# Attention run ahead of the weights, chunk six spread behind the last weights, and the products of chunks four and five gathered by batch

## The chip, the cores and the metric

One Trainium2 chip, of which the kernel uses one core. A core has a matrix engine (TensorE; PE in the profile, PEld for its weight loads), VectorE (DVE), ScalarE (ACT), GpSimd (POOL), and SyncE (SP), which here only issues transfers. They run side by side and wait for each other through semaphores; 16 DMA engines move data between main memory and the on-chip memory. POOL issues all loads here, since they convert float32 to 16 bits on the way; SP issues the rest. The metric is device time in microseconds (us) for one execution.

## The reference

A causal attention with a cumulative bias, and on its result a spectral mixing layer with 64 complex weight matrices. B = 8 batches, H = 8 heads, S = 576 tokens, head width 64, model width 512:

```python
scores = scale * np.matmul(q, k.transpose(0, 1, 3, 2))
cum = np.cumsum(np.maximum(s, 0.0), axis=-1)
bias = -(cum[:, :, :, None] - cum[:, :, None, :])
scores = np.where(causal, -1e9, scores + np.minimum(bias, 0.0))
attn = softmax(scores)
x = heads_side_by_side(np.matmul(attn, v))        # [8, 576, 512]

X = np.fft.rfft(x, axis=1)                        # 64 modes are kept
Yr = einsum('bmd,mde->bme', Xr, w_r) - einsum('bmd,mde->bme', Xi, w_i)
Yi = einsum('bmd,mde->bme', Xr, w_i) + einsum('bmd,mde->bme', Xi, w_r)
y = np.fft.irfft(Y, n=S, axis=1)
u = x + y
return u + np.maximum(u @ w_ch, 0.0)
```

The two weight tensors w_r and w_i are 64 x 512 x 512 each, 134 MB together in float32; q, k and v are 9.4 MB each. The output is 9.4 MB.

## The kernel before, in words

**Steps and groups.** Attention runs in 32 steps (line 591). Step n takes two heads (group n // 8, 128 of the 512 columns) of batch n % 8: `scores` (lines 391 and 397 on TensorE, the exponentials of line 405 and, for the last 64 tokens, 376 on ScalarE), `av` (line 433, normalised into x_all in line 443), and `fft`, the forward transform of the step's columns into 64 modes (line 458), copied to `xs` (line 468). The next step's q and k are transposed on the way (line 355, copies of line 359).

**Units and chunks.** The weights come in 64 units: a group's 128 rows of eight modes of w_r or of w_i, 1.05 MB on chip, two loads of 512 KB (the very last unit four of 256 KB). A chunk is the two units of eight modes: 32 chunks, eight for each of the four groups. `modes` multiplies a chunk (line 478): 16 products, four at a time side by side in the array; the sums over the groups gather in y_acc. The last group's eight chunks are called chunk zero to chunk seven below (24 to 31 of 32 in all); their sum is y for eight modes, 16 rows (real and imaginary) of each batch. A chunk needs attention to have finished its group for all eight batches.

**Where the weights wait.** The first four units lie in space that is used later for other things. From then on two rings hold them: five buffers (WA) and three (WB), the ring of three only up to unit 37 (LW2). A unit's load waits until the chunk that last used its buffer is multiplied. `on_chip` says how many half units are asked for by step n, and `mode_steps` in which step which chunk is multiplied. POOL issues the loads strictly in the order of the program: step n asks for v of step n + 3, for q and k of steps n + 3 and n + 4 in odd steps, and for weights, evenly mixed (`load`, line 244). In `before` 51 units are asked for by step 31, and 24 chunks are multiplied during attention. Counted off from the program:

| by step | 8 | 16 | 24 | 31 |
|---|---|---|---|---|
| units asked for, before | 12 | 24 | 40 | 51 |
| chunks multiplied before that step, before | 0 | 8 | 16 | 23 |

**Behind attention.** The remaining chunks are multiplied as their units land. Beside them the kernel works ahead on the product x @ w_ch. The output is made in 18 pairs of 128-token tiles. For 16 of them (`kept`) x @ w_ch is stored: the tile is transposed (line 669, copied by DVE in line 673), multiplied with w_ch (line 682) and stored by ScalarE (line 539). `work` does one transposition of a pair and the product and storing of the pair before; `TAKE` says how many turns of it come after which chunk. In `before`, six of these pairs (`first_pairs`) are done earlier, in attention's steps 26 to 31 (lines 548, 553, 571), and ten behind it: three, two and three turns after chunks zero, one and two, and two inside the first gather; the last pair is kept in the middle of chunk six.

**From y to the inverse transform.** The inverse transform needs, for each batch, the 128 mode rows of y and of v = y @ w_ch below each other, in `yv`; y itself leaves `modes` with eight batches mixed in its rows. Two ways lead there. `gather` does it with TensorE: the transposed y (line 702) times an identity (for y) or times w_ch (for v), separately for each batch, and copies from the accumulators by ScalarE and VectorE (lines 739 and 741). The other way is `spread` (line 513), a transfer of SP, 128 KB. In `before` chunks zero to three are gathered after chunk three, both y and v, in four rounds of two batches; y of chunks four and five is gathered after chunk five, in two rounds of four batches; v of four and five (multiplied for all batches at once in line 710) and y and v of six and seven are spread.

**The end.** While chunk seven's last unit arrives, `first_z` and `first_u` begin the first two pairs; chunks six and seven enter these pairs directly (line 785), for all others they come from yv. Then the list of steps at the end of the function finishes the 18 pairs in an order written out by hand: products of line 774 and 804, a ReLU or copy on ScalarE (825, 827), sums on DVE and POOL, outputs by SP.

SP's queue holds in order: small loads of bias rows in attention, constants, the spreads, the outputs.

Of the kernel before, what the change touches and what calls it, by code (L numbers as in the profile page):

```python
# [10 lines left out]
FP32 = mybir.dt.float32  # L11
# [8 lines left out]
def kernel(  # L20
# [83 lines left out]

    xs = [gp.tile([P, 2, 2, 2, 2, B, HM], BF16, name=f"xs{i}") for i in range(2)]
    xs_flat = [t.rearrange("p q k h r b m -> p (q k h r b m)") for t in xs]
# [9 lines left out]

    dpool = ctx.enter_context(tc.tile_pool(name="dram", bufs=1, space=bass.MemoryType.DRAM))
    ncum_dram = dpool.tile([NPAIR, S + HP], BF16, name="ncum_dram")
    at = ExitStack()
# [128 lines left out]
    NW = 2  # L248
    mode_steps = {B: [0, 1, 2, 3], B + 1: [4], B + 2: [5], B + 4: [6], B + 6: [7]}
    for c in range(NCK, (NG - 1) * NCK):  # L250
        mode_steps.setdefault(B + c - (0 < c % NCK < 4), []).append(c)
    used = [NW * sum(len(cs) for t, cs in mode_steps.items() if t < n) for n in range(N + 1)]
    W0 = 2
    on_chip = []
    for n in range(N):
        w = 4 + 2 * (WA + WB + NE - 2) * (n + 1) // (B + 1) if n < B else plan + (3 if n <= 2 * B else 4)
        plan = w

        nt, ring = 0, ([], [])
        while nt < min(w // 2, len(wq)):  # L260
            i = ring_of(nt)
            if i is not None:
                depth = (WA, WB)[i]
                if len(ring[i]) >= depth and ring[i][-depth] >= used[n]:
                    break
                ring[i].append(nt)
            nt += 1
        if nt < w // 2:
            plan = 2 * nt + 1
        on_chip.append(2 * nt)  # L270

# [178 lines left out]
    def fft(n):  # L450
# [13 lines left out]
        for h in range(2):  # L464
            for q_ in range(2):
                a = ps[HP * q_ : HP * q_ + HP, h, : 2 * HM].rearrange("p (r m) -> p r m", r=2)
                a = bass.AP(tensor=a.tensor, offset=a.offset, ap=[a.ap[0], [HM, 2]] + list(a.ap[1:]))
                nc.vector.tensor_copy(out=xs[g % 2][HP * h : HP * h + HP, q_, :, h, :, b, :], in_=a)  # L468

    def modes(g, c, meanwhile=None):  # L470


        ps = auxpool.tile([P, DM], FP32, name="yp", tag="aux")
        cols = xs[g % 2].rearrange("p q k h r b m -> p q k (h r b) m")

# [21 lines left out]
        elif g < NG - 1:  # L497
            nc.vector.tensor_tensor(out=y_acc[:, c, :], in0=ps, in1=y_acc[:, c, :], op=ALU.add)  # L498
        else:
            yb = spool.tile([P, DM], FP16, name="y_sb", tag="y")  # L500
            for cols in halves if c == NCK - 1 else [slice(0, DM)]:
                nc.vector.tensor_tensor(
                    out=yb[:, cols], in0=ps[:, cols], in1=y_acc[:, c, cols], op=ALU.add
                )
            if c >= NCK - 2:
                spread(c, 0, yb)
            return yb
# [18 lines left out]

    first_pairs = [i for i in kept[1:] if pairs[i][0][1] < NF and pairs[i][0][0] <= 4][:6]
    z1s, xts1 = {}, {}

# [13 lines left out]

    def first_transposed(i, x):
        b, T = pairs[i][x]
        ps = auxpool.tile([P, DT, P], FP32, name="xt_ps", tag="aux")
        for dt in range(DT):
            nc.tensor.matmul(
                ps[:, dt, :], x_all[:, dt, b, T, :], ident16h, start=True, stop=True,
                skip_group_check=True,  # L550
            )
        xts1[i, x] = spool.tile([P, DT, P], FP16, name="xt1", tag="yt")
        nc.vector.tensor_copy(out=xts1[i, x], in_=ps)

    open_unit = {}

    def half_of(pool, name):
# [6 lines left out]
        return t[:, :HU]  # L564

    def first_product(i, x):
        if x == 0:
            kept_place(i, half_of(wpool2, "z1"))
        ps = auxpool.tile([P, DM], FP32, name="z1_ps", tag="aux")
        for dt in range(DT):  # L570
            nc.tensor.matmul(
                ps, xts1[i, x][:, dt, :], wch_sb[:, dt, :], start=(dt == 0), stop=(dt == DT - 1)
            )
        keep_product(i, x, ps)


# [5 lines left out]
    with tc.tile_pool(name="sc_psum", bufs=2, space=PSUM) as scpool, \  # L582
# [8 lines left out]
        for n in range(N):  # L591
            if n in (0, 2):
                nc.vector.memset(xs_flat[n // 2].bitcast(FP32), 0.0)
# [18 lines left out]
            scores(n, 1)  # L612
            i = first_pairs[n - N + len(first_pairs)] if n >= N - len(first_pairs) else None
            if i is not None:
                first_transposed(i, 0)
            transposes(n + 1, 1)
            fft(n - 1)
            av(n, 0)
            if i is not None:
                first_product(i, 0)  # L620
                first_transposed(i, 1)
            if i is not None:
                first_product(i, 1)
        av(N - 1, 1)
# [17 lines left out]

    NLOC = 5
    old = xs_flat[0]
    xt_sb = [
# [4 lines left out]

    places = [finpool.tile([P, 4 * DM], BF16, name="r_sb", tag="r", bufs=3) for i in range(2)]
    places += [finpool.tile([P, 4 * DM], BF16, name=f"z1_{i}") for i in range(NLOC)]
    places.append(old[:, 4 * DM : 8 * DM])
    places += [y_acc[:, c : c + 2, :].rearrange("p c e -> p (c e)").bitcast(BF16) for c in (0, 2)]
# [32 lines left out]
    def keep(i):  # L687
        x_times_wch(i, True)
        j = late.index(i)
        kept_place(i, places[j])  # L690
        for x in range(2):
# [15 lines left out]
    def y_times_wch(c, yt):  # L707
# [6 lines left out]
        nc.vector.tensor_copy(out=vb, in_=vp)  # L714
        spread(c, 1, vb)
        return vb

    def gather(c0, c1, turns, kinds):

# [3 lines left out]
        for b0 in range(0, B, ng):  # L723
            for which in kinds:
                ps = auxpool.tile([P, DM], FP32, name="g_ps", tag="aux")
                for dt in range(DT):
# [9 lines left out]
                for g in range(ng):  # L736
                    dst, src = yv[rows, b0 + g, which, :], ps[n * g : n * g + n, :]
                    if g % 2:
                        nc.vector.tensor_copy(out=dst, in_=src)
# [19 lines left out]

    late = [i for i in kept if i not in first_pairs]  # L760
    order_z = late[:-1]
    TAKE = (3, 2, 3, 0, 0, 0)
    us, rs = {}, {}
# [120 lines left out]
    yb6 = modes(NG - 1, c, {2: lambda: keep(late[-1])})  # L884
    x_times_wch(1, False, (0,))
# [113 lines left out]
```

## Time and profile before

| | |
|---|---|
| three timed runs | 440.73, 440.25, 440.62 us; median 440.62 |
| the profiled execution | 440.91 us |
| its span, first to last instruction | 439.1 us |
| mean granted TensorE clock | 0.909 of full |

Busy time by engine, from the first part of the page: the share of the span and the number of instructions.

```profile
PE 344.2 (78%) x4409; PEld 205.8 (47%) x4409; DVE 252.3 (57%) x574; ACT 226.0 (51%) x421; POOL 171.4 (39%) x257
```

Queues: q0 are POOL's loads, q1 SP's transfers. The last column is the time of their packets as a share of 16 engines' span; it can pass 100% since packets overlap.

```profile
q0 software_dynamic: 61424, 81.28, 104.9%
q1 hardware_dynamic: 6936, 11.14, 7.0%
```

The chain that ended last, by engine:

```profile
DMA 52%; PE 25%; DVE 14%; issue 4%; POOL 2%; ACT 2%; DVEq 0%; POOLq 0%; ACTq 0%
```

How to read it: busy shares are averages over stages with different limits. Attention and the mode products fill the first 330 us, the remaining chunks run until 405 us, and the outputs from 410 to 438 us. What a change in a stage is worth is read from what that stage waits for last.

### The profile page before, as it was taken

The page shows a single profiled execution, that of the slowest core. Times are in us where ns is not written, and L with a number is a line of the kernel's source. Part 1 is how long each engine was busy: PE and PEld are TensorE (multiplying, and loading weights), DVE is VectorE, ACT ScalarE, POOL GpSimd, SP SyncE. Part 2 cuts the span into 40 slices and gives each one's busy share as a digit, 9 for nine tenths or more (in the row PEclk, how much of TensorE's full clock was granted, in tenths as well). Part 3 has the DMA queues.
Part 4 walks back from the last instruction along what each step waited for, and adds up shares of the span by engine and source line. Part 5 has one row for each costly group of instructions (what it writes and reads, how often), then busy time and mean ns, then how long its engine had stood idle before and what let it go on. Part 6 is the DMA issues. An engine that isn't in the chain of part 4 may idle for free.

```text
span 439.1 us, 10583 instructions
## 1 busy us (share of the span) xinstructions
PE 344.2 (78%) x4409; PEld 205.8 (47%) x4409; DVE 252.3 (57%) x574; ACT 226.0 (51%) x421; POOL 171.4 (39%) x257
## 2 busy tenths in 40 slices
PE   1598899899695977983938548889996986769994
PEld 1365566466463534651615225555653544433441
DVE  7667776677564545672624325666655542462795
ACT  1386888268563724760725124566661442422794
POOL 6555444344354443423434334433322221130293
PEclk9998999999987969895877866999997996999999
DMA  8999999999999999999999999999999999997498
GB/s 162 207 205 207 204 206 208 207 209 207 208 206 206 209 207 210 208 209 209 205 209 209 209 208 207 207 209 206 212 211 212 211 211 211 201 208 154 160 381 345
DMA packets 68407, 93.09 MB, mean 212 GB/s; under 512 B 25276, under 2 KB 27064, under 8 KB 68360
## 3 DMA queue, kind: packets, MB, share of 16 engines
q0 software_dynamic: 61424, 81.28, 104.9%
q1 hardware_dynamic: 6936, 11.14, 7.0%
q8 instruction: 34, 0.56, 0.5%
q14 instruction: 13, 0.11, 0.1%
HBM read 163.37 MB, written 9.51 MB: 394 GB/s over the span
## 4 chain that ended last, share of the span: by engine, by line
DMA 52%; PE 25%; DVE 14%; issue 4%; POOL 2%; ACT 2%; DVEq 0%; POOLq 0%; ACTq 0%
DMA w_sb<-in_moe_w_r_dram 24%; DMA w_sb<-in_moe_w_i_dram 16%; DMA qk<-in_k_dram 8%; PE yp L478 3%; PE z_ps L682 3%; DMA qk<-in_q_dram 3%; DVE qt L359 3%; PE sc_ps L397 3%; DVE xs L468 2%; PE av_ps L433 2%; DVE x_all L443 2%; PE sc_ps L391 2%; PE tr_ps L355 2%; PE g_ps L729 2%; DMA v<-in_v_dram 2%
## 5 line engine op out<-in xcount | busy, mean ns | idle before, releaser
L405 ACT ACTIVATE p_sb<-sc_ps,cumt_sb 128x576 f16<-128x576 f32 (+1 forms) x256 | 141.9, 635 | 22.6 <-PE sc_ps L397 22.1
L397 PE MATMUL sc_ps<-qt,kt 128*128 128x512 bf16 (+2 forms) x384 | 78.7, 318 | 6.3 <-ACT kt L359 5.6
L244 POOL DMA_DIRECT2D v<-in_v_dram x72 | 51.3, 714 | 60.3 <-DMA w_sb<-in_moe_w_r_dram 11.6
L244 POOL DMA_DIRECT2D w_sb<-in_moe_w_i_dram x62 | 38.4, 621 | 89.7 <-PE yp L478 30.3
L359 DVE COPY qt<-tr_ps 64x576 bf16<-64x576 bf16 x64 | 47.8, 746 | 42.3 <-PE tr_ps L355 42.3
L478 PE MATMUL yp<-w_sb,xs 128*32 128x512 bf16 (+1 forms) x480 | 42.7, 434 | 26.9 <-DMA w_sb<-in_moe_w_i_dram 23.4
L355 PE MATMUL tr_ps<-ident,qk 64*64 64x64 bf16 x1152 | 34.8, 206 | 32.3 <-DMA qk<-in_k_dram 15.2
L244 POOL DMA_DIRECT2D w_sb<-in_moe_w_r_dram x60 | 37.3, 623 | 53.6 <-DMA w_sb<-in_moe_w_r_dram 32.9
L397 PEld LDWEIGHTS <-kt 128*128 128x128 bf16 x384 | 39.0, 106 | 35.0 <-ACT kt L359 12.2
L391 PE MATMUL sc_ps<-negm,ident 128*128 128x256 bf16 x256 | 54.6, 299 | 0.0
L355 PEld LDWEIGHTS <-qk 64*64 64x64 bf16 x1152 | 26.8, 119 | 50.3 <-DVE kt L359 19.5
L376 ACT ACTIVATE p<-sc_ps,cumt 128x64 f16<-128x64 f32 x32 | 10.0, 313 | 74.2 <-PE sc_ps L372 74.2
L433 PE MATMUL av_ps<-v,p_sb 128*128 128x65 f16 x1024 | 44.7, 198 | 1.9 <-DVE x_all L443 0.7
L359 ACT COPY kt<-tr_ps 64x576 bf16<-64x576 bf16 x32 | 22.8, 713 | 40.8 <-DVE qt L359 40.1
L433 PEld LDWEIGHTS <-p_sb 128*128 128x128 f16 x1024 | 38.0, 100 | 9.8 <-DVE x_all L443 5.6
L468 DVE CAST xs<-ft_ps 64x128 bf16<-64x128 f32 x128 | 36.7, 287 | 6.9 <-PE ft_ps L458 5.5
L438 DVE TENSOR_REDUCE den<-av_ps 128x5 f32<-128x10 f32 x64 | 10.8, 169 | 49.9 <-PE av_ps L433 48.9
L478 PEld LDWEIGHTS <-xs 128*32 128x32 bf16 (+1 forms) x512 | 17.4, 145 | 44.7 <-DMA w_sb<-in_moe_w_i_dram 26.0
L443 DVE TENSOR_TENSOR x_all<-av_ps,rcp 128x320 f16<-128x320 f32 x64 | 31.5, 491 | 2.2
L498 DVE TENSOR_TENSOR y_acc<-yp,y_acc 128x512 f32<-128x512 f32 x16 | 11.1, 691 | 28.8 <-PE yp L478 28.0
L458 PE MATMUL ft_ps<-Ff_sb,x_all 128*64 128x192 f16 (+1 forms) x320 | 24.2, 264 | 1.0 <-DVE x_all L443 1.0
L359 DVE COPY kt<-tr_ps 64x576 bf16<-64x576 bf16 x32 | 24.4, 763 | 0.4
(110 smaller groups left out, 429.5 us busy)
## 6 DMA issues: line engine op xcount, KB each, us to landing
w_sb<-in_moe_w_r_dram POOLq DMA_DIRECT2D x60, 512.0 KB, 13.5
w_sb<-in_moe_w_i_dram POOLq DMA_DIRECT2D x55, 512.0 KB, 13.2
out_dram<-r_w SPq DMA_DIRECT2D x16, 512.0 KB
v<-in_v_dram POOLq DMA_DIRECT2D x72, 64.0 KB, 11.1
qk<-in_q_dram POOLq DMA_DIRECT2D x15, 288.0 KB, 11.9
qk<-in_k_dram POOLq DMA_DIRECT2D x15, 288.0 KB, 13.2
x_all<-in_moe_w_r_dram POOLq DMA_DIRECT2D x4, 512.0 KB, 8.8
w_sb<-in_moe_w_i_dram POOLq DMA_DIRECT2D x3, 384.0 KB, 12.7
```

Source lines behind the costliest of these rows:

```text
L244: nc.gpsimd.dma_start(out=dst, in_=src)
L355: nc.tensor.transpose(ps[rows, r, :], src[rows, r, :], ident16[rows, rows])
L359: copy(out=to[:, :, :, half * RH : half * RH + RH], in_=ps[HP * i : HP * i + HP].rearrange("d r (h p) -> d h p r", h=2),)
L391: nc.tensor.matmul(ps[:, bass.ds(w * S, W)], ident16, negm[:, bass.ts(r, W)], start=True, stop=False, skip_group_check=True,)
L397: nc.tensor.matmul(ps[:, c0 : c0 + i1 - i0], keys[:, w, r, :], qh[:, i0:i1], start=False, stop=True, skip_group_check=True,)
L405: nc.scalar.activation(out=pt[:, poff[x] : poff[x] + S - w * W], in_=ps[:, w * S : (w + 1) * S - w * W], func=ACTF.Exp, bias=cumt_sb[:, x, ...
L433: nc.tensor.matmul(ps[:, I, r : r + NCH], lhsT, rhs, start=(i == 0), stop=(i == len(todo) - 1), skip_group_check=True,)
L443: nc.vector.tensor_tensor(out=x_all[:, g, b, :, D * h : D * h + D], in0=ps[:, :, 1 : NCH], in1=rcp.unsqueeze(2).to_broadcast([P, NT, D]), ...
L458: nc.tensor.matmul(ps[HP * q_ : HP * q_ + HP].rearrange("p h f -> p (h f)"), x_all[:nT, g, b, T, q_::2], Ff_sb[:nT, T, :], start=(T == 0), ...
L468: nc.vector.tensor_copy(out=xs[g % 2][HP * h : HP * h + HP, q_, :, h, :, b, :], in_=a)
L478: nc.tensor.matmul(ps[32 * cg : 32 * cg + 32, :], cols[k0:, q_, 1 - ri, :, c * MC // 2 + cg], wt[(g, c, ri)][cg // 2][k0:, 2 * (cg % 2) + ...
L682: nc.tensor.matmul(zs[i, x], xts[i][:, x, dt, :], wch_sb[:, dt, :], start=(dt == 0), stop=(last and dt == DT - 1), skip_group_check=True,)
```

## The change

Three things change in the program.

1. *Order of loads and of work.* `on_chip` follows a plain rule, about one unit a step, and `mode_steps` a list. By step 31 37 units are asked for, and 17 chunks are multiplied during attention (the last in step 30); the other 15 follow it. Since groups now overlap in time, `xs` gets a third buffer (XS). The six pairs done in attention's last steps are done behind it too: `first_transposed` and `first_product` go, and 16 turns of `work` stand after chunks 18 to 23 and 25 of 32; the last pair is kept after chunk five. The stored products lie in other places (three buffers of the weights' second ring, xs, y_acc and buffers of their own).
2. *v of chunks four and five.* The second gather makes y and v, v first; its second round uses another accumulator pool; which engine copies is chosen by kind. The products of line 710 for these two chunks and their two spreads go. The first gather has no turns of `work` inside it.
3. *Spreads of chunk six.* Its y and v are no longer spread as soon as they are there. SP first issues a transfer of four bytes that reads the last unit's buffer, and so waits for the last load; the two spreads stand behind it in SP's queue.

| by step | 8 | 16 | 24 | 31 |
|---|---|---|---|---|
| units asked for, after | 12 | 21 | 30 | 37 |
| chunks multiplied before that step, after | 0 | 8 | 13 | 17 |

```diff
-    xs = [gp.tile([P, 2, 2, 2, 2, B, HM], BF16, name=f"xs{i}") for i in range(2)]
+    xs = [gp.tile([P, 2, 2, 2, 2, B, HM], BF16, name=f"xs{i}") for i in range(3)]
+    XS = (0, 1, 2, 0)
...
+    mark = dpool.tile([1, 2], BF16, name="mark")
...
-    mode_steps = {B: [0, 1, 2, 3], B + 1: [4], B + 2: [5], B + 4: [6], B + 6: [7]}
-    for c in range(NCK, (NG - 1) * NCK):
-        mode_steps.setdefault(B + c - (0 < c % NCK < 4), []).append(c)
+    mode_steps = {
+        B: [0, 1, 2, 3], 9: [4], 10: [5], 12: [6], 14: [7], 16: [8], 18: [9], 19: [10], 21: [11], 23: [12],
+        25: [13], 26: [14], 28: [15], 30: [16],
+    }
+    done = [c for t in sorted(mode_steps) for c in mode_steps[t]]
...
-        w = 4 + 2 * (WA + WB + NE - 2) * (n + 1) // (B + 1) if n < B else plan + (3 if n <= 2 * B else 4)
...
+        w = 3 + n if n < B else 4 + n + (n - B) // B
...
+        on_chip.append(2 * w)
...
-            if c >= NCK - 2:
+            if c >= NCK - 1:
                 spread(c, 0, yb)
...
-            i = first_pairs[n - N + len(first_pairs)] if n >= N - len(first_pairs) else None
-            if i is not None:
-                first_transposed(i, 0)
             transposes(n + 1, 1)
             fft(n - 1)
             av(n, 0)
-            if i is not None:
-                first_product(i, 0)
-                first_transposed(i, 1)
-            if i is not None:
-                first_product(i, 1)
...
-        spread(c, 1, vb)
+        if c < NCK - 2:
+            spread(c, 1, vb)
...
-    def gather(c0, c1, turns, kinds):
+    def gather(c0, c1, turns, kinds, then=None):
...
-                ps = auxpool.tile([P, DM], FP32, name="g_ps", tag="aux")
+                pool, tag = then if then and b0 else (auxpool, "aux")
+                ps = pool.tile([P, DM], FP32, name="g_ps", tag=tag)
...
-                    if g % 2:
+                    if (which == 0 and (b0 == 0 or g < 2)) if then else g % 2:
                         nc.vector.tensor_copy(out=dst, in_=src)
...
-    late = [i for i in kept if i not in first_pairs]
+    late = list(kept)
...
-    TAKE = (3, 2, 3, 0, 0, 0)
+    TAKE = {18: 3, 19: 3, 20: 3, 21: 3, 22: 1, 23: 2, 25: 1}
...
+    for c in range(len(done), (NG - 1) * NCK):
+        modes(c // NCK, c % NCK)
+        for x in range(TAKE.get(c, 0)):
+            work()
     for c in range(NCK - 2):
         yb = modes(NG - 1, c)
-        for x in range(TAKE[c] - 1):
-            work()
         if c == NCK - 3:
             x_transposed(late[-1])
             x_transposed(0)
         yt = y_transposed(yb, c)
-        if TAKE[c]:
+        for x in range(TAKE.get((NG - 1) * NCK + c, 0)):
             work()
         if c >= NY:
             if c == NCK - 3:
                 x_times_wch(0, False)
                 x_transposed(1)
-            y_times_wch(c, yt)
             if c == NCK - 3:
-                gather(NY, NCK - 2, (), (0,))
+                keep(late[-1])
+                gather(NY, NCK - 2, (), (1, 0), (upool, "u"))
         elif c == NY - 1:
-            gather(0, NY, (1, 3), (1, 0))
+            gather(0, NY, (), (1, 0))
     assert not order_z and not ahead
     c = NCK - 2
-    yb6 = modes(NG - 1, c, {2: lambda: keep(late[-1])})
+    yb6 = modes(NG - 1, c)
...
+    nc.sync.dma_start(
+        out=mark[:1], in_=wt[(NG - 1, NCK - 1, 1)][1][HP : HP + 1, WM - 1, :2]
+    )
+    spread(c, 0, yb6)
+    spread(c, 1, vb6)
```

More of the change, by code (lines that the diff above doesn't have):

```diff
@@ L255 @@
     for n in range(N):
-        w = 4 + 2 * (WA + WB + NE - 2) * (n + 1) // (B + 1) if n < B else plan + (3 if n <= 2 * B else 4)
[L257 to L261, printed above, removed]
-            if i is not None:
[L263 to L270, printed above, removed]
+        w = 3 + n if n < B else 4 + n + (n - B) // B
+        for u in range(NE, w):
+            ring = [x for x in range(NE, u + 1) if ring_of(x) == ring_of(u)]
+            depth = (WA, WB)[ring_of(u)]
+            assert len(ring) <= depth or ring[-1 - depth] < used[n], (n, u)
+        on_chip.append(2 * w)
     nc.sync.dma_start(out=s_sb, in_=s.rearrange("b h t -> (b h) t"))
@@ L467, in fft @@
                 a = bass.AP(tensor=a.tensor, offset=a.offset, ap=[a.ap[0], [HM, 2]] + list(a.ap[1:]))
-                nc.vector.tensor_copy(out=xs[g % 2][HP * h : HP * h + HP, q_, :, h, :, b, :], in_=a)
+                nc.vector.tensor_copy(out=xs[XS[g]][HP * h : HP * h + HP, q_, :, h, :, b, :], in_=a)
     def modes(g, c, meanwhile=None):
         ps = auxpool.tile([P, DM], FP32, name="yp", tag="aux")
-        cols = xs[g % 2].rearrange("p q k h r b m -> p q k (h r b) m")
+        cols = xs[XS[g]].rearrange("p q k h r b m -> p q k (h r b) m")
         def product(ri, q_, cg):
@@ L525 @@
     ways = dict(zip(kept, "vsgmsgsgmsgsgsgs"))
-    first_pairs = [i for i in kept[1:] if pairs[i][0][1] < NF and pairs[i][0][0] <= 4][:6]
-    z1s, xts1 = {}, {}
+    z1s = {}
     def kept_place(i, t):
@@ L542, in keep_product @@
         nc.vector.tensor_tensor(out=z1s[i][:, 1, xx], in0=z, in1=z1s[i][:, 0, xx], op=ALU.subtract)
[L544 to L553, printed above, removed]
     open_unit = {}
@@ L564, in half_of @@
         return t[:, :HU]
[L566 to L574, printed above, removed]
     def mode_products(n, half=None):
@@ L591 @@
         for n in range(N):
-            if n in (0, 2):
+            if n in (0, 2, 4):
                 nc.vector.memset(xs_flat[n // 2].bitcast(FP32), 0.0)
@@ L618 @@
             av(n, 0)
-            if i is not None:
-                first_product(i, 0)
-                first_transposed(i, 1)
-            if i is not None:
-                first_product(i, 1)
         av(N - 1, 1)
@@ L641 @@
     upool = xt.enter_context(tc.tile_pool(name="u_psum", bufs=2, space=PSUM))
-    NLOC = 5
-    old = xs_flat[0]
+    NLOC = 3
+    old = xs_flat[1]
     xt_sb = [
@@ L649 @@
     xt_sb.append(finpool.tile([P, 2, DT, P], FP16, name="xt_x"))
-    places = [finpool.tile([P, 4 * DM], BF16, name="r_sb", tag="r", bufs=3) for i in range(2)]
+    places = [lambda: half_of(wpool2, "z1")] * (2 * WB)
+    places.append(old[:, 4 * DM : 8 * DM])
+    places += [finpool.tile([P, 4 * DM], BF16, name="r_sb", tag="r", bufs=3) for i in range(2)]
     places += [finpool.tile([P, 4 * DM], BF16, name=f"z1_{i}") for i in range(NLOC)]
-    places.append(old[:, 4 * DM : 8 * DM])
+    places += [xs_flat[2][:, i * 4 * DM : (i + 1) * 4 * DM] for i in range(2)]
     places += [y_acc[:, c : c + 2, :].rearrange("p c e -> p (c e)").bitcast(BF16) for c in (0, 2)]
@@ L689, in keep @@
         j = late.index(i)
-        kept_place(i, places[j])
+        kept_place(i, places[j]() if callable(places[j]) else places[j])
         for x in range(2):
@@ L758, in work @@
             keep(i)
-    late = [i for i in kept if i not in first_pairs]
+    late = list(kept)
+    assert len(places) == len(late)
     order_z = late[:-1]
-    TAKE = (3, 2, 3, 0, 0, 0)
+    TAKE = {18: 3, 19: 3, 20: 3, 21: 3, 22: 1, 23: 2, 25: 1}
     us, rs = {}, {}
```

## The prediction, made before the changed kernel ran

> **What bounds the kernel now.** I read the page's slices first, then the chain of waits, then TensorE's and POOL's rows in order of time over the last 80 us, then TensorE's granted clock over stretches of 3.41 us. The page shows a kernel bound by its loads:
>
> ```profile
> PEclk9998999999987969895877866999997996999999
> DMA  8999999999999999999999999999999999997498
> GB/s 162 207 205 207 204 206 208 207 209 207 208 206 206 209 207 210 208 209 209 205 209 209 209 208 207 207 209 206 212 211 212 211 211 211 201 208 154 160 381 345
> ```
>
> The DMA engines are full from 10 us to 400 us; 52% of the chain is DMA. The 154 to 160 GB/s behind it is the turn from the last weights to the first outputs. Such a kernel gains only if fewer bytes or holes stand before the last weights, or if less work follows them, and the work beside them must keep up. Does it? I took TensorE's rows; from 363 us on they read (start, length, line; in brackets what ended the idle time before):
>
> ```profile
> 363.69 0.66 PE L478 MATMUL yp<-w_sb,xs 128*32 128x512 bf16 x8 [2.07 <-DMA w_sb<-in_moe_w_i_dram]
> 366.22 1.99 PE L729 MATMUL g_ps<-wch_sb,yt_first 128*64 128x512 f16 x8 [0.68 <-ACT yt_first L704]
> 369.60 1.98 PE L729 MATMUL g_ps<-wch_sb,yt_first 128*64 128x512 f16 x8 [0.95 <-DVE yv L739]
> ...
> 374.63 1.14 PE L729 MATMUL g_ps<-wch_sb,yt_first 128*64 128x512 f16 x8
> ...
> 377.17 1.14 PE L729 MATMUL g_ps<-wch_sb,yt_first 128*64 128x512 f16 x8 [0.99 <-DVE yv L739]
> ...
> 380.48 1.09 PE L478 MATMUL yp<-w_sb,xs 128*32 128x512 bf16 x16
> ...
> 384.47 1.09 PE L478 MATMUL yp<-w_sb,xs 128*32 128x512 bf16 x16
> ...
> 405.22 0.65 PE L478 MATMUL yp<-w_sb,xs 128*32 128x512 bf16 x4
> ```
>
> The rows of L478 are the mode products of the last group's chunks three (363.69), four, five and, at 405.22, the last quarter of chunk seven. At 405.22 the last weights have just landed (the DMA share is 0.05 until 405.0), yet TensorE had been busy since 394.72 with gaps under 2 us: loads and TensorE arrive together. Whatever makes either later is paid in full. The four rounds of the first gather (L729) are what to look at: the same eight products take 1.99 us in two of them and 1.14 in the others. The clock tells why (stretch, its length, TensorE busy, granted clock, DMA share, GB/s):
>
> ```profile
> 359.25:362.66 3.41, 2.37 (x16) 1.00 1.12 210
> 362.66:366.08 3.42, 1.05 (x12) 0.99 1.12 211
> 366.08:369.49 3.41, 2.42 (x16) 0.50 1.12 211
> 369.49:372.90 3.41, 3.30 (x25) 0.51 1.12 211
> 372.90:376.32 3.42, 3.28 (x25) 1.00 1.12 211
> ...
> 379.73:383.14 3.41, 2.24 (x24) 1.00 1.07 201
> ```
>
> After a stretch with TensorE 31% busy the next one has half the clock; after one 71% busy it stays at half; after 97% it is back. Other stretches of this trace: 49% (134 to 137 us) fell, 61% (393 to 397) did not; 87% (264 to 267) did not bring it back once, and did once (339 to 342). So: below about half it falls, and about nine tenths restore it.
>
> **The parts and their prices.**
>
> *Order of loads.* The bytes ahead of the last product are the same but for the spreads. By the POOL order of the new kernel, step 31 has asked for 37 units of weights (two loads of 512 KB each) where before it was 51, so attention ends near 260 us. A step needs one unit and its q, k, v: 1.49 MB, at 207 GB/s 7.2 us. Its work takes 6.63 us (the rows of L376 lie at 50.14, 56.77, 63.39), and a chunk adds 1.03: over steps 9 to 31 with 13 chunks also 7.2. v is asked for three steps ahead, some 20 us of cover. Bounds: nothing, and, were each step 5% longer, 23 x 0.36 = 8 less part of the cover, say 5. I take nothing; the stretch from 20 to 80 us ran at this density with 204 to 208 GB/s.
>
> *Work moved behind attention.* Six pairs' transposes and products (L548, L571) leave steps 26 to 31; 16 turns of `work` now lie in chunks 18 to 25 of 32. A turn costs TensorE 2.4 us (346.83 to 349.24), three and a chunk 8.4, and two units take 9.9 at 211 GB/s: hidden. So is the third buffer's memset (1.77 us of DVE in step 4, as the two others were). But from chunk 24 on only one half turn is left where before there were ten with the gather's: TensorE then works some 2 us in 10, far under half of a stretch, and meets the gather at half clock.
>
> *First gather, no turns in it.* Four rounds at half clock: 369.60 - 366.22 = 3.38 each, 13.5 in all. Each is busy 2.42 of 3.38 us, 72%, so by the stretches above it never comes back; before, the turn at 371.95 filled one. Chunk three's products and transposes at half clock add 0.7 ahead: start 366.9, end 380.4. Chunk four begins as before (380.48), though two turns are gone.
>
> *Chunks four and five.* Chunk four at half clock: 1.09 x (1.99/1.14 - 1) = +0.8, its transposes +0.2. Its own product with w_ch (L710) and the wait for it, 382.77 to 384.46, are gone: -1.7. So chunk five starts at 383.8 instead of 384.46: -0.7; its second unit lands then too (368.96 and three units of 4.98). Still at half clock: its products +0.8, transposes +0.2 (the four DVE casts of 0.61 hide the rest), the product of pair 0 (1.90) +1.4, and half of what follows until a stretch is filled, +0.7: +3.1. Ends: one such stretch only, +1.3; three, +4.2. The rest at full clock: the kept pair is only moved (it stood inside chunk six); v by batch costs two products of about 1.0 for one of 1.04; the casts now run on ACT (10 x 0.58) and DVE (6 x 0.69) side by side instead of in turn, but chunk six's sum on DVE waits behind them. Laying these rows end to end from chunk five's start gives 21.0 us to the last quarter, against 405.22 - 384.46 = 20.8: +0.2.
>
> [...]
>
> *Spreads.* Chunk six's two and the v of four and five, 128 KB each, no longer stand between weights. Unit 60 landed at 388.8 (POOL's last issue waits for it, eight issues on), 63 at 405.0:
>
> ```profile
> 368.96 0.61 POOL L244 DMA_DIRECT2D w_sb<-in_moe_w_r_dram  x1 [1.68 <-DMA w_sb<-in_moe_w_r_dram]
> 382.85 1.22 POOL L244 DMA_DIRECT2D w_sb<-in_moe_w_i_dram  x2 [13.28 <-PE yt_ps L702]
> ...
> 388.85 0.59 POOL L244 DMA_DIRECT2D w_sb<-in_moe_w_i_dram  x1 [1.61 <-DMA w_sb<-in_moe_w_r_dram]
> ```
>
> From unit 56 to 60 a unit took 4.98; three of them 14.9, but 16.2 passed: 0.43 for each of the three spreads in it. Four removed: the last weights land 1.7 us earlier, at 403.4. Worth -1.7 only if TensorE is there, and it isn't. The marker holds SP until that landing; behind it stand both spreads of six (0.55 issue each), those of seven and all outputs. Seven's sum comes about 1.5 us after the last quarter, when the queue is empty again: nothing; without that cover at most 0.55.
>
> *Sum.* -0.7 + 3.1 + 0.2 = +2.6: the last quarter at 407.8, and behind it the same 33.9 us of finishing. Span 439.1 + 2.6 = 441.7; the profiled run's 440.91 and the median's 440.62 differ by 0.3, so I add the 2.6 to the median: **443.2 us**, own range 441.9 to 444.8.
>
> **Rivals.**
> - *TensorE keeps its clock* (one mechanism, at chunks three to five): then the gather ends by 377, chunk five starts as its weights land, 383.4, and the last quarter comes at 383.4 + 20.5 = 403.9, half a microsecond behind the last landing. -1.3: 439.3, faster. It decides as soon as the stretches around the gather are nine tenths full, or where busy TensorE rows and the gate's own measure differ. For it: two restorations near 0.87 to 0.91. Against: 0.72 is clear of both.
> - *The clock comes back inside the gather* but is lost again in the 3 us wait before chunk five, one stretch at half: +1.3 on -1.3: 440.6, no change.
> - *Attention starves the loads*: DMA slices under 200 GB/s between 100 and 260 us, +5 on top of the landing: 445.5. The slices at 20 to 80 us speak against.
> - *The spreads don't do what is said*: the marker waits for one load, the last; if others trail, the spreads cut in again, 0.9 us of the 1.7, and no effect while TensorE is last.
>
> **Numbers.** Forecast 0.55, clock kept 0.26, clock back 0.13, starved 0.06. About 0.2% (0.9 us) is what a measurement can tell from no change: faster 0.26, same 0.14, slower 0.60. The range reaches from the kept clock's 439.3, with half a microsecond of its own, to the forecast's upper end: 438.8 to 444.8; it leaves out the starved case and the faster cases' tail.
>
> **What would show it.** Right: in the new profile the clock at half from about 355 to 390 us, four gather rounds near 3.4 us, chunk five's products near 384 taking about 2 us, the last quarter waiting for nothing at about 408 while the last weights landed near 403.5. Wrong: gather rounds of 2.5 us, a wait for weights before the last quarter, or thin DMA slices before 260 us.

## The result, and the profile after

| | before | changed |
|---|---|---|
| first comparison, median and extremes | 440.44 (440.24 to 440.73), 4 runs | 443.20 (442.04 to 444.37), 4 runs |
| the same again, on the chip of the last four experiments | 440.57 (439.33 to 444.71), 31 runs | 443.04 (440.87 to 445.51), 8 runs |
| profiled execution, its span | 440.91, 439.1 | 442.04, 440.1 |
| mean granted TensorE clock | 0.909 | 0.901 |

The changed kernel takes 1.0062 of the time before (95% interval 1.0034 to 1.0090), the second time 1.0055 (1.0030 to 1.0080): 2.5 to 2.8 us more. The forecast of 443.2 is met to the tenth. That is luck in good part, as the trace shows. First the slices of the changed kernel's page:

```profile
PEclk9999999999999699999699996999957555599997
DMA  9999999999999999999999999999999999995597
GB/s 168 208 206 206 205 206 208 206 209 208 204 205 208 208 209 208 202 206 209 208 208 209 196 212 211 211 211 211 211 211 211 211 211 211 211 211 101 207 396 281
```

The half clock is there, from 336 to 387 us, and the DMA engines stay full to the end of the loads: 211 GB/s in every slice from the 25th to the 36th. But the last slice moves 281 GB/s where it moved 345 before. Next TensorE's rows of the changed kernel in order of time (start, length, line; L473 is the line called L478 before, L697 was L729):

```profile
362.03 1.09 PE L473 MATMUL yp<-w_sb,xs 128*32 128x512 bf16 x8 [3.83 <-DMA w_sb<-in_moe_w_i_dram]
...
365.19 1.98 PE L697 MATMUL g_ps<-wch_sb,yt_first 128*64 128x512 f16 x8 [0.68 <-ACT yt_first L670]
...
368.57 1.98 PE L697 MATMUL g_ps<-wch_sb,yt_first 128*64 128x512 f16 x8 [0.96 <-DVE yv L707]
...
378.70 1.94 PE L473 MATMUL yp<-w_sb,xs 128*32 128x512 bf16 x16 [0.95 <-DVE yv L707]
...
381.97 1.94 PE L473 MATMUL yp<-w_sb,xs 128*32 128x512 bf16 x16
...
404.38 0.65 PE L473 MATMUL yp<-w_sb,xs 128*32 128x512 bf16 x4
```

The gather's rounds are 3.38 us apart, four take 13.51 us, and chunks four and five take 1.94 us each: as forecast. Yet the last quarter of chunk seven comes at 404.38, not at 407.8, and 0.84 us earlier than before (405.22). The span is 1.0 us longer all the same. So in this execution everything that was lost was lost behind the last quarter: 440.1 - 404.4 = 35.7 us, where it had been 439.1 - 405.2 = 33.9. The end of the changed kernel by stretches of a microsecond (the engines' busy times, granted clock, DMA share, GB/s):

```profile
435.00:436.00 1.00, 0.00 (x0) 0.00 (x0) 0.00 (x0) 0.00 (x0) 0.00 (x0) 0.51 1.05 406
436.00:437.00 1.00, 0.00 (x0) 0.00 (x0) 0.00 (x0) 0.00 (x0) 0.00 (x0) 0.50 0.83 316
437.00:438.00 1.00, 0.00 (x0) 0.00 (x0) 0.00 (x0) 0.00 (x0) 0.00 (x0) 0.50 0.06 25
438.00:439.00 1.00, 0.00 (x0) 0.00 (x0) 0.00 (x0) 0.00 (x0) 0.00 (x0) 0.50 0.05 18
```

All outputs were issued 0.8 us earlier than before, and at 436.8 nearly all have ended. Then a DMA share of 0.06, one engine of 16, goes on alone until 438.7. What held it back is in the queues of the stretch from 427 to 434 us (packets, MB, time as a share of 16 engines):

```profile
q1 hardware_dynamic: 1423, 2.75, 102.0%
q8 instruction: 1, 0.02, 1.6%
```

q8 carries code: one packet of 16 KB, started at 427.62, that took 1.74 us (1.6% of 16 engines for 7 us). The outputs keep all 16 engines full there (102.0% in that stretch, a share of 1.05 from 435 to 436 us), and one engine ends 1.9 us behind the others (436.8 to 438.7). The trace doesn't name the engine of a packet; that the one which trails is the one that carried the code, and trails because of it, is inferred. All engines also dip for a moment in that stretch, to 152 GB/s in one slice of 0.175 us; what makes the dip isn't shown. In the trace of before the last packet of code started at 408.39, when little else was moving (a DMA share of 0.24 from 408 to 410 us). Its stretch from 427 to 434 us has none and no dip, and its engines stop together, here in stretches of half a microsecond:

```profile
q1 hardware_dynamic: 1486, 2.85, 105.2%
```

```profile
437.00:437.50 0.50, 0.00 (x0) 0.00 (x0) 0.00 (x0) 0.00 (x0) 0.00 (x0) 1.00 0.95 365
437.50:438.00 0.50, 0.00 (x0) 0.00 (x0) 0.00 (x0) 0.00 (x0) 0.00 (x0) 0.69 0.05 16
438.00:438.50 0.50, 0.00 (x0) 0.00 (x0) 0.00 (x0) 0.00 (x0) 0.00 (x0) 0.50 0.00 0
```

Counted in the trace, these packets come at every 254th record of TensorE on the mean (products, weight loads and a few others). Single gaps run from 162 to 352 records in the two traces. Before, the 34th came at record 8637 of 8889; by the mean, as an estimate, a 35th was due at record 8891, just behind the program's end. The changed kernel has 56 more records, 48 of them the products and weight loads of v by batch, and so a 35th packet, at record 8890 of 8945.

### The profile page after: what moved, and what is told of

Its sections match the earlier page's. It is cut to its first block, busy times and chain, and to the rows that moved or that the text cites. A ratio compares the mean times of both kernels' runs of the same rounds, so it can differ in the third digit from the quotient of the medians.

```text
span 440.1 us, 10666 instructions
## 1 busy us (share of the span) xinstructions
PE 343.4 (78%) x4433; PEld 202.7 (46%) x4433; DVE 253.6 (58%) x575; ACT 229.4 (52%) x427; POOL 171.3 (39%) x257
## 4 chain that ended last, share of the span: by engine, by line
DMA 55%; PE 20%; DVE 15%; ACT 5%; issue 3%; POOL 1%; DVEq 0%; POOLq 0%
DMA w_sb<-in_moe_w_i_dram 30%; DMA w_sb<-in_moe_w_r_dram 17%; DMA qk<-in_q_dram 7%; DVE qt L354 3%; PE yp L473 3%; PE sc_ps L392 2%; PE g_ps L697 2%; DVE xs L463 2%; ACT yv L709 2%; PE av_ps L428 2%; DVE x_all L438 2%; PE tr_ps L350 2%; DVE kt L354 2%; PE z_ps L743 2%; PE u_ps L773 2%
## 5 line engine op out<-in xcount | busy, mean ns | idle before, releaser
L392 PE MATMUL sc_ps<-qt,kt 128*128 128x512 bf16 (+2 forms) x384 | 73.2, 301 | 7.8 <-ACT kt L354 5.8
L473 PE MATMUL yp<-w_sb,xs 128*32 128x512 bf16 (+1 forms) x480 | 46.8, 469 | 38.5 <-DMA w_sb<-in_moe_w_i_dram 29.2
L392 PEld LDWEIGHTS <-kt 128*128 128x128 bf16 x384 | 36.1, 101 | 35.0 <-ACT kt L354 15.8
L386 PE MATMUL sc_ps<-negm,ident 128*128 128x256 bf16 x256 | 51.7, 285 | 0.2
L350 PE MATMUL tr_ps<-ident,qk 64*64 64x64 bf16 x1152 | 31.9, 200 | 20.7 <-DVE kt L354 19.5
L428 PE MATMUL av_ps<-v,p_sb 128*128 128x65 f16 x1024 | 43.5, 196 | 3.5 <-issue 1.6
L473 PEld LDWEIGHTS <-xs 128*32 128x32 bf16 (+1 forms) x512 | 18.2, 147 | 60.2 <-issue 29.6
L428 PEld LDWEIGHTS <-p_sb 128*128 128x128 f16 x1024 | 36.3, 99 | 11.8 <-DVE x_all L438 5.9
L350 PEld LDWEIGHTS <-qk 64*64 64x64 bf16 x1152 | 24.6, 113 | 34.4 <-DVE kt L354 26.3
L497 DVE TENSOR_TENSOR y_sb<-yp,y_acc 128x512 f16<-128x512 f32 (+1 forms) x9 | 5.6, 631 | 39.4 <-PE yp L473 39.3
L533 ACT COPY z<-z_ps 128x512 f32<-128x512 f32 x18 | 10.6, 586 | 30.0 <-PE z_ps L648 18.4
```

Source lines behind the costliest of these rows:

```text
L350: nc.tensor.transpose(ps[rows, r, :], src[rows, r, :], ident16[rows, rows])
L386: nc.tensor.matmul(ps[:, bass.ds(w * S, W)], ident16, negm[:, bass.ts(r, W)], start=True, stop=False, skip_group_check=True,)
L392: nc.tensor.matmul(ps[:, c0 : c0 + i1 - i0], keys[:, w, r, :], qh[:, i0:i1], start=False, stop=True, skip_group_check=True,)
L428: nc.tensor.matmul(ps[:, I, r : r + NCH], lhsT, rhs, start=(i == 0), stop=(i == len(todo) - 1), skip_group_check=True,)
L473: nc.tensor.matmul(ps[32 * cg : 32 * cg + 32, :], cols[k0:, q_, 1 - ri, :, c * MC // 2 + cg], wt[(g, c, ri)][cg // 2][k0:, 2 * (cg % 2) + ...
```

## The experiments

Three theories for the 2.5 to 2.8 us. *Code*: the 35th packet, some 1.8 us. *Clock*: the half clock, with TensorE last from chunk five on, as forecast. *Marker and spreads*: the transfers' new places. Times before are the medians of the runs beside each set, 440.43 (four experiments), 440.54 (four) and 440.57 (four).

### The code's boundary moved, in both directions

The changed kernel with 88 products added in step 0, where TensorE waits for a copy; they write an accumulator that nothing reads.

```diff
         transposes(0, 0)
+        spare(88)
         transposes(0, 1)
```

> The changed kernel with 88 small products on TensorE added in step 0, where TensorE waits 3.64 us for a copy (176 instructions; nothing reads them). [...] 176 instructions earlier in the program is about 408.5 us, where the DMA engines are nearly idle: no fetch after 410, the last packets of outputs at 436.8, span 1.7 to 1.9 us shorter beyond what the added products cost at the start (0 to 1 us): 440.9 to 442.2 against 443.2. Rival (the tail has another cause, the marker or the DMA state): one engine still trails to 438.7, the time is 443.2 or up to 1 us more. The clock of TensorE from 337 to 386 us stays at half in either.

Measured 441.56 (440.26 to 443.61, 12 runs), ratio 1.0020 (1.0002 to 1.0038): 1.5 to 1.6 us less than the changed kernel, by adding work. (The intervals overlap a little, up to 1.0038 here and from 1.0030 there, so the size is less sure than the direction.) The last packet of code starts at 410.97. Its queues from 427 to 434 us, and its end:

```profile
q1 hardware_dynamic: 1481, 2.85, 105.2%
```

```profile
437.00:438.00 1.00, 0.00 (x0) 0.00 (x0) 0.00 (x0) 0.00 (x0) 0.00 (x0) 1.00 1.06 408
438.00:439.00 1.00, 0.00 (x0) 0.00 (x0) 0.00 (x0) 0.00 (x0) 0.00 (x0) 0.87 0.64 244
```

The engines stop together, none trails. The profiled execution took no less than the changed kernel's, because here the clock cost more (last quarter at 406.36). Behind it stand 440.28 - 406.36 = 33.9 us, the length of before.

The kernel before, with 30 such products (`spare(30)`):

> The kernel before with 30 of the same small products in step 0 (60 instructions of TensorE). Code theory: its program ends some four instructions before a 35th fetch would come; 60 more bring that fetch to about 428 us, in the full outputs, as in the changed kernel: one DMA engine trails the others by 1.5 to 2 us at the end, time 441.9 to 442.6 against 440.5, with the last quarter of chunk seven still at about 405.2. Rival (code fetches cost nothing there): 440.4 to 440.9.

Measured 442.26 (441.38 to 445.23, 11 runs), 1.0040 (1.0021 to 1.0059): +1.8 us for 60 instructions of TensorE at the very start. No trace shows the four instructions of the expectation; by the mean of 254 records it is an estimated two. The 35th packet started at 428.15 and took 1.64 us; the last quarter came at 404.80, 35.7 us before the end. The same end as in the changed kernel, in a kernel without any of the change:

```profile
437.00:438.00 1.00, 0.00 (x0) 0.00 (x0) 0.00 (x0) 0.00 (x0) 0.00 (x0) 0.50 0.43 164
438.00:439.00 1.00, 0.00 (x0) 0.00 (x0) 0.00 (x0) 0.00 (x0) 0.00 (x0) 0.50 0.06 25
439.00:440.00 1.00, 0.00 (x0) 0.00 (x0) 0.00 (x0) 0.00 (x0) 0.00 (x0) 0.50 0.01 4
```

### The second part alone

The kernel before with v of chunks four and five by batch, and the gather's new argument that goes with it:

```diff
...
-            y_times_wch(c, yt)
             if c == NCK - 3:
-                gather(NY, NCK - 2, (), (0,))
+                gather(NY, NCK - 2, (), (1, 0), (upool, "u"))
```

> The kernel before with the second part of the change alone: v of chunks four and five made by batch in the second gather, their product of line 710 and their two spreads gone. TensorE gets 48 instructions more. Code theory: that is enough for a 35th fetch, near 429 us in the full outputs, one DMA engine trails by 1.5 to 2 us, 441.9 to 442.8 against 440.4. Rival (the part is priced by its work on TensorE alone, two products of 1.05 us for two of 1.04, and two spreads of 0.43 us less before the last weights): 440.2 to 440.8.

Measured 441.91 (440.35 to 443.28, 12 runs), 1.0024 (1.0007 to 1.0040): +1.4 us. The packet is there, at 429.55. With `spare(88)` besides:

> The same with 88 small products more in step 0, so that TensorE's last code fetch comes 176 instructions earlier, near 410 us, ahead of the full outputs. Code theory: no engine trails, the difference to the kernel with the second part alone is 1.4 to 2.0 us: 440.0 to 441.0. Rival (fetches are not it): the same time as the kernel with the second part alone.

Measured 440.81 (439.58 to 442.56, 12 runs), 1.0005 (0.9990 to 1.0020): no change from before can be told. The difference of the two, 1.1 us, is under the 1.4 to 2.0 expected. The packet of the first took only 0.88 us, yet behind the last quarter it has 35.38 us against 34.05 in the second: a packet's own time doesn't give its price. So v by batch costs or gains nothing that these runs can tell, but for the 35th packet that it brings.

The traces together give the packet's price. From the start of the last quarter to the end of the span:

| | us |
|---|---|
| last packet of code before 412 us: kernel before, code moved, second part and code moved, products in the waits (below), less work behind chunk five without the marker (below) | 33.92, 33.92, 34.05, 33.94, 33.98 |
| a packet at 427 to 430 us: changed kernel (twice), before with 30 products, second part alone, and three more below | 35.75, 35.58, 35.69, 35.38, 35.64, 35.57, 35.96 |

One more trace with an early packet, that of less work behind chunk five with the marker, has 34.79 us; 0.79 us of them are a wait for a spread, which is shown there.

### The third part undone

Chunk six's spreads issued at once, no marker:

```diff
-    nc.sync.dma_start(
-        out=mark[:1], in_=wt[(NG - 1, NCK - 1, 1)][1][HP : HP + 1, WM - 1, :2]
-    )
-    spread(c, 0, yb6)
-    spread(c, 1, vb6)
...
-            if c >= NCK - 1:
+            if c >= NCK - 2:
                 spread(c, 0, yb)
...
-        if c < NCK - 2:
-            spread(c, 1, vb)
+        spread(c, 1, vb)
```

> The changed kernel with chunk six's two spreads issued as soon as their rows are there, as before, and no marker. Theory (TensorE comes last, so what the loads win isn't used): the last weights land 0.8 to 0.9 us later, near 403.5 instead of 402.6, the last quarter stays where TensorE's own work puts it, 442.9 to 443.5, within 0.3 of the changed kernel. Rival (the loads set the end): 0.8 us slower, 444.0. Rival (the marker costs time in SP's queue, since the spreads of six wait for the last load): 0.5 us faster, 442.7 or less.

Measured 443.22 (441.98 to 444.12, 6 runs), 1.0048 (1.0031 to 1.0066): the same as the changed kernel. The first theory's time held, but not its landing: the spreads went out at 398.59 and 401.76, among the last loads, and the last packet of weights ended at 402.30, against 402.51 behind the marker. By these two traces two spreads in the way cost the loads nothing.

### The turns put back

The changed kernel with two of its turns in the first gather again (`gather(0, NY, (1, 3), (1, 0))`, one less after chunks 20 and 21):

> The changed kernel with two of the 16 turns moved from chunks 20 and 21 into the first gather, after its first and third round, as before. Clock theory: the gather still starts near 365.2 at half clock with rounds of 3.4 us, the first turn fills a stretch of 3.41 us and full clock is back by 373; chunk four starts near 379.5, chunk five near 382, both at full clock (1.09 us of products), chunk five to the last quarter 20.8 us instead of 22.4, so the last quarter at 402.9 to 403.4, after a short wait for the last weights (402.8): 1.0 to 1.5 us less than the profiled run of the changed kernel, 441 to 442 in the median, and a smaller scatter than 442.0 to 444.4. The code fetch in the outputs stays, about 427. Rival (the half clock costs nothing that matters, the loads or the copies set the end): last quarter at 404.4, time 443.2 with the same scatter.

Measured 442.76 (441.69 to 443.75, 10 runs), 1.0049 (1.0033 to 1.0066): 0.3 to 0.4 us less, which isn't clear of the scatter. Full clock was back at 375 us, and from chunk five to the last quarter it took 21.1 us instead of 22.4; but chunk five began at 383.93 instead of 381.97, since the gather had started 1.3 us later in this execution (366.50 against 365.19) and the turns took the rest. The last quarter came at 405.04: a gain in the rate, given back in the start. Then with all turns late:

```diff
-    TAKE = {18: 3, 19: 3, 20: 3, 21: 3, 22: 1, 23: 2, 25: 1}
+    TAKE = {18: 2, 20: 2, 22: 1, 23: 1, 24: 3, 25: 2, 26: 3}
...
-            gather(0, NY, (), (1, 0))
+            gather(0, NY, (1, 3), (1, 0))
```

> The changed kernel with its 16 turns put as late as before: two, two, one and one after chunks 18, 20, 22 and 23, three, two and three after 24, 25 and 26, two inside the first gather. Clock theory: full clock from 335 to 366 us as in the kernel before, the gather from 365.2 with two cold and two warm rounds, chunk four near 379.5, chunk five near 382, the last quarter at 402.9 to 403.4 behind the last weights; 441 to 442, as with the two turns alone, since the part before the gather isn't on the path. If the half clock before 365 us costs as well, this kernel is faster than the one with two turns moved by 0.3 us or more. Rival: 443.2, last quarter 404.4.

Measured 442.29 (440.71 to 443.47, 12 runs), 1.0035 (1.0020 to 1.0050). Full clock through the gather, in rounds of 2.54 us; then chunk five's second half waited 2.32 us for its weights, until 382.47, the clock fell at 383.7 for two stretches, and the last quarter came at 405.50. So the clock was lost in the wait before chunk five, as the second rival of the prediction has it, but for two stretches where the rival named one. The same with `spare(88)`:

> The changed kernel with its turns as late as before and 88 small products in step 0, but the last pair left where the change put it, behind chunk five. If the two causes add up (code fetch 1.6, turns 0.9): 442.3 - 1.6 = 440.4 to 440.9. The 0.5 to 0.9 us between this and the kernel that also moved the last pair (439.97) is then what the 3 us of work taken from behind chunk five are worth. Rival (the fetch and the clock overlap, only one counts): 441.3 to 441.8.

Measured 441.92 (440.23 to 587.41, 12 runs; without the one far outside, up to 443.55), 1.0022 (1.0005 to 1.0039). 0.4 us less than without the added products, where 1.6 were expected, and no better than the code moved alone. The sum of the two causes didn't come: once the code is moved, these intervals can't tell that the late turns are worth anything. The only trace of this kernel is of the execution far outside, so it doesn't show where the time went.

### The changed kernel once more

It was measured again beside the kernels that follow:

> The changed kernel once more, for a median over more than four runs on the chip and at the time of the next three: 443.0 to 443.5 by either theory, 35th code fetch near 427, half clock from 337 to about 386 us.

Measured 443.04 (440.87 to 445.51, 8 runs), the second row of the table above. The packet came at 427.56, the last quarter at 404.31.

### The clock alone

The clock was then held without moving any work, again by 88 products that nothing reads: 29 of the small ones in step 0, and 59 larger ones (128 by 512) in TensorE's waits around the first gather and chunk five.

```diff
+        if c == NY - 1:
+            fill(6)
+        n_fill = {NY - 1: 14, NCK - 3: 20}.get(c, 0)
-        yb = modes(NG - 1, c)
+        yb = modes(NG - 1, c, {2: lambda: fill(n_fill)} if n_fill else None)
...
+        if c == NY - 1:
+            fill(3)
...
+            if not then:
+                fill(4)
```

> The changed kernel with the same 88 products added as in the run with the code moved, but 59 of them (128 by 512, read by nothing) put where TensorE waits: 6 before chunk three, 14 between its halves, 3 behind it, 4 after each round of the first gather, 20 between the halves of chunk five; the other 29 in step 0. Same length of code, so the last fetch again near 410 us; the order of all real work is the changed kernel's. Clock theory: full clock from about 360 to 405 us, gather rounds of 2.5 us, chunk five's second half as its weights land, 382.4 to 383.5, 20.8 us to the last quarter, at 403.2 to 404.3; with 33.9 us behind it 438.6 to 440.0 and less scatter, against 441.6 with the code moved alone. Rival (the half clock costs nothing on the path): 441.2 to 441.9.

Measured 441.00 (439.68 to 442.78, 12 runs), 1.0008 (0.9993 to 1.0023): 0.6 us less than the code moved alone, where some 2 us were expected; the intervals overlap. TensorE's rows of this kernel:

```profile
365.32 1.14 PE L704 MATMUL g_ps<-wch_sb,yt_first 128*64 128x512 f16 x8
...
372.94 1.14 PE L704 MATMUL g_ps<-wch_sb,yt_first 128*64 128x512 f16 x8
...
383.36 0.67 PE L479 MATMUL yp<-w_sb,xs 128*32 128x512 bf16 x8 [0.52 <-DMA w_sb<-in_moe_w_i_dram]
383.96 0.62 PE L642 MATMUL xt_ps<-ident16h,x_all 128*128 128x128 f16 x8
...
404.07 0.65 PE L479 MATMUL yp<-w_sb,xs 128*32 128x512 bf16 x4
```

The row at 383.36 is chunk five's second half, that of L642 the first transposes behind it. With the code moved alone these come at

```profile
384.23 1.03 PE L642 MATMUL xt_ps<-ident16h,x_all 128*128 128x128 f16 x8
```

From them to the last quarter it is 20.1 us here (to 404.07) and 22.1 there (to 406.36): behind chunk five the half clock cost 2.0 us there, and in the changed kernel's two executions, with 20.5 and 20.1, at most 0.4. Ahead of chunk five the rounds of 2.54 us bring chunk four 3.5 us earlier (375.47 against 378.93), and of that 0.3 us are left at the transposes. The rest is spent in waiting for chunk five's weights: its second half can't start before they land, at 382.5 in the kernel with late turns and 383.3 here.

### Less work behind chunk five

If TensorE's work from chunk five on is what the end waits for, less of it must help, whatever the clock. The late turns, `spare(88)`, and the last pair's and the first pair's transposes and the last pair's products moved from behind chunk five to ahead of it:

```diff
-        if c == NCK - 3:
-            x_transposed(late[-1])
-            x_transposed(0)
         yt = y_transposed(yb, c)
+        if c == NCK - 4:
+            x_transposed(late[-1])
+            x_transposed(0)
+            keep(late[-1])
...
-                keep(late[-1])
                 gather(NY, NCK - 2, (), (1, 0), (upool, "u"))
```

> The changed kernel with its turns as late as before (three, two and three after chunks 24, 25 and 26, two in the first gather), the last pair's transposes and product and the first pair's transposes moved ahead of chunk five into its 2.3 us wait for weights, and 88 small products in step 0 for the code fetch. Theory (TensorE's 21 to 23 us of work from chunk five on is what the end waits for, and the half clock makes it longer): chunk five's second half near 383, at most 19 us of work behind it, so the last quarter now waits for the last weights (402.6 to 402.9) and comes at 403.2 to 403.8; with 33.9 us behind it 438.7 to 439.3. Rival (the work moved only shifts the wait, the clock falls again before chunk five): last quarter at 404.5 to 405.5, 440 to 441.

Measured 439.97 (439.29 to 441.33, 12 runs), 0.9985 (0.9973 to 0.9996): 3.1 to 3.2 us under the changed kernel and 0.6 under the kernel before, and the executions lie closer together. Against the same kernel without the moved work (late turns and code moved, 441.92) it is 1.9 us less, and these two intervals lie apart: TensorE's work behind chunk five is on the path. TensorE now waits for the last weights:

```profile
383.02 1.10 PE L479 MATMUL yp<-w_sb,xs 128*32 128x512 bf16 x16
...
403.36 0.65 PE L479 MATMUL yp<-w_sb,xs 128*32 128x512 bf16 x4 [0.31 <-DMA w_sb<-in_moe_w_i_dram]
...
409.25 0.62 PE L750 MATMUL u_ps<-yv,G_sb 128*64 128x512 f16 x4 [0.79 <-DMA yv<-y_sb]
```

The last quarter came as expected, the time is 0.7 us over its range, and the last row says why: a wait of 0.79 us for the spread of chunk seven's y, which SP sent at 405.01 right behind the two spreads of six that the marker had held until 403.64. Here, with TensorE early, the marker is in the way. So without it:

> The kernel with late turns, the last pair ahead of chunk five and the code moved, now with chunk six's two spreads issued at once and no marker. There SP sent them at 403.6 and 404.3, just ahead of chunk seven's y at 405.0, and TensorE waited 0.8 us at 409.3 for that y. Theory (the spreads took nothing from the loads, and behind the marker they now stand in the way): the last weights land within 0.3 us of 403.0, no wait for y, the first output 0.5 to 0.8 us earlier: 439.2 to 439.6. Rival (each spread costs the loads 0.43 us): last weights at 403.8, 440.0 to 440.8.

Measured 439.98 (439.31 to 440.90, 11 runs), 0.9989 (0.9970 to 1.0008): no gain. The wait for y is gone, but in its profiled execution the last weights landed at 403.92 instead of 402.98, about what the rival named (403.8). The same spreads took nothing in the experiment on the third part, so this trace alone can't tell whether they or the later chunk four (378.56 against 377.09) made the loads late. That stays open.

## Why the prediction was right in its time, and where its steps failed

*The clock, as forecast.* The four rounds took 13.51 us for 13.5; from chunk four to five it was 3.27 for 3.4. The clock did what was read from the trace before. Stretches of the changed kernel (TensorE busy, granted clock, DMA share, GB/s):

```profile
373.59:377.00 3.41, 2.46 (x19) 0.50 1.13 211
377.00:380.41 3.41, 2.46 (x26) 0.50 1.12 211
380.41:383.83 3.42, 2.63 (x24) 0.50 1.11 209
383.83:387.24 3.41, 2.97 (x26) 0.50 1.12 211
387.24:390.65 3.41, 3.41 (x30) 1.00 1.12 211
```

Six stretches in a row, 64 to 77% busy, restored nothing (the last three are shown); the one that was 87% busy did.

*Start of the gather: 1.7 us off.* Forecast 366.9, measured 365.19. I took the landing of chunk three's last load, 363.69, from the one execution before. Two kernels with that order of loads had it at 362.31 and 363.30, the changed kernel at 362.03: an execution's scatter, taken for a fixed point.

*From chunk five to the last quarter: the term "+3.1" was mis-sized.* Forecast 20.8 + 0.2 + 3.1 = 24.1 us; measured 22.4 and 22.0 in two executions of the changed kernel, 23.6 with the spreads at once, 24.2 with the code moved. So in place of 3.1 the term was 1.4 and 1.0, then 2.6 and 3.2; one of the four lies under the lower end I gave (+1.3 to +4.2). Where it falls is decided at a stretch on the edge: with the code moved, the stretch from 384.09 to 387.50 was busy for 2.97 us too, and didn't restore the clock.

```profile
384.09:387.50 3.41, 2.97 (x25) 0.50 1.12 211
387.50:390.91 3.41, 3.41 (x14) 0.50 1.12 211
```

*Spreads: the price of 0.43 us was wrong.* I laid 1.3 us between the landings of units 60 and 63 on three spreads. They were the hole in the loads from 382 to 386 us, in these stretches of the trace before:

```profile
380.00:382.00 2.00, 1.57 (x19) 0.57 (x17) 0.63 (x2) 0.90 (x2) 0.00 (x0) 1.00 1.13 212
382.00:384.00 2.00, 0.90 (x7) 0.49 (x8) 0.31 (x1) 0.58 (x1) 1.15 (x2) 1.00 0.86 161
384.00:386.00 2.00, 2.00 (x27) 1.06 (x26) 1.08 (x2) 0.00 (x0) 1.85 (x4) 1.00 1.06 172
```

(51 + 40) of 212 GB/s for 2 us are 0.9 us of loading, the larger part of it. I had shown the row with its cause, POOL waiting 13.28 us until TensorE freed chunk four's buffers at 382.85, and read past it. In the changed kernel POOL waits until 380.11 and the hole is gone (210 to 212 GB/s): that, more than the spreads, is why the weights land at 402.5. The two kernels with the second part say the same: with the hole (175 and 183 GB/s) the last packet of weights ended at 404.24, without it at 403.04, and the same two spreads of six stood in both. For the two spreads of v that are gone in both, at most the 0.4 us from 404.62 before to 404.24 are left. That the weights land early isn't used, as forecast, for TensorE is last.

*"Behind it the same 33.9 us of finishing": the step that failed.* It was 35.7. The term had been carried over as a constant, and the 48 instructions that I priced by their time on TensorE alone brought a 35th packet of code, 1.4 to 2.0 us at the end of the traces. So the sum should have been made of two parts: by the medians 1.5 to 1.8 us for the packet (two pairs of kernels; the pair with the second part alone gave 1.1, and the pair with late turns only 0.4, of whose kernels one has no trace to compare; where both kernels have one, the ends differ by 1.3 to 1.8), and about 1 us for all the rest of the change (the code moved: 441.56, 1.1 us over before). That the rest is the half clock is supported by the traces, in which TensorE comes last and its stretch from chunk five on is 1.2 to 3.4 us longer than before. It isn't shown by the times: holding the clock won 0.6 us, with overlapping intervals. Over the changed kernel's twelve executions the three with a mean clock above 0.9 took 440.87 to 442.04 us, the nine from 0.891 to 0.896 took 441.83 to 445.51; over the twelve with the code moved no such order is seen. The cause of this last 1 us stays open. Errors of -3.4 us at the last quarter and +1.8 behind it met the scatter of the executions, whose median lies 1.2 us above the profiled one; so the right total came about, by luck.

*Attention ahead of the weights* cost the loads nothing that shows: one slice of 196 GB/s lies near its end, and from the next on all have 211 or 212 until the loads run out.

*The packet of code.* The traces show its size, 16 KB, and its place, every 254 records on the mean. Among saturated outputs (383 to 411 GB/s from 426 to 434 us) the end came 1.4 to 2.0 us later.

## What to carry to other kernels

Where the end of a kernel is a stretch of saturated transfers, look at when the last packets of code are fetched: here 60 instructions more in the first step of the program moved one in, for 1.8 us, and 176 more moved one out of the changed kernel, for 1.5 to 1.6 us less, though nothing reads what they compute. Before an edit is priced by the engine that it is on, ask which work stands behind the last of several loads: here 3 us of TensorE's work moved ahead of a wait were worth 1.9 us, more than the clock, the turns and the spreads. And a fixed point taken from one execution (a landing, the length of the end) should carry its scatter into the sum.

## What the runs showed of the hardware

- Sixty instructions of TensorE in step 0, in a wait, made a kernel 1.8 us slower; 176 made another 1.5 to 1.6 us faster. With a packet of code among the outputs one DMA engine's worth of work went on alone at the end (share 0.06), in the two traces without one whose ends are shown none did. A packet of code took 0.89 to 0.98 us in 67 of the 69 cases in the traces before and after, 1.27 us at 408.39 before, and 0.88, 1.64 and 1.74 us among the outputs of three kernels.
- In the traces before and after the granted clock changed only in steps of 3.41 us, between 1.0 and 0.5. It fell behind stretches of 3.41 us with TensorE 0 to 54% busy before and 23 to 66% busy after, and held behind others with 43 to 68%. Half clock ended behind stretches that were 87 to 100% busy; behind those of 86% or less it stayed, and so it did behind one of 99% (335.29 us, before).
- At 87% busy (2.97 of 3.41 us) the clock was restored in the changed kernel's execution (383.83 to 387.24), and not with the code moved (384.09 to 387.50).
